# FFN2 in column groups of 256 and 512 in a fused attention and FFN kernel, with the bursts and the loads reordered

## The chip, the cores and the metric

The kernel runs on one core of a Trainium2 chip. The core has a matrix engine (TensorE, PE in the profile; its weight loads are listed as PEld), a vector engine (VectorE, DVE), a scalar engine (ScalarE, ACT), a general engine (GpSimd, POOL) and a sync engine (SP). In this kernel POOL only starts loads, and SP only starts transposes and the writes of the output. The metric is the time of one execution on the device in microseconds (us), lower is better; the time before is 387.18 us, the median of four runs from 386.85 to 387.43.

## What is computed

The reference is an attention without softmax, followed by a feed-forward network with a leaky activation:

```python
scores = (q @ k^T) / sqrt(64)                # 8 batches, 12 heads, 448 x 448
attn   = maximum(scores, 0)**2 / 448
x      = concat_heads(attn @ v)              # 3584 tokens x 768
h      = x @ w_in                            # 768 -> 2048
g      = maximum(h, 0) + alpha * minimum(h, 0)
out    = g @ w_out                           # 2048 -> 768, float32
```

All inputs are float32 in HBM. The loads that POOL starts convert to bfloat16 on the way, and the matrix products are done in bfloat16 with float32 sums.

## The kernel before

**Attention in quads.** Four heads of one batch make a quad; there are 24, three to a batch, numbered 0 to 23. `load_qk` (L93) and `load_v` (L102) bring a quad's q, k and v into SBUF through POOL. q and k must then be turned so that the head's 64 dimensions lie along the partitions. For quads 0 to 4 `turn_pe` (L148) does it with TensorE; from quad 5 on `turn_dma` (L160) does it: two DVE copies reorder q and k into a tile `perm`, then one DMA transpose issued by SP writes the tile `T`. The raw tiles of q and k have three buffers each, so a load of quad n waits until the tiles of quad n - 3 have been turned.

A quad's scores come in seven chunks. `score_mm` (L172) runs four matmuls of 64 x 64 weights by 448 columns for a chunk, side by side in the four quarters of the array, into a pair of PSUM banks. `relu` (L183) takes the chunk out of PSUM on ACT or DVE, and `square` (L191) squares it in SBUF. `attnv` (L199) runs 28 matmuls, seven rounds of four, over the seven squared chunks, again into a pair of banks, and ACT (L216) and DVE (L217) each take one bank of it out, scaled, into `xT`.

**FFN1** (`f1_mm` L238, `f1_out` L244): for each batch, 16 blocks `ff` of 128 hidden features, six matmuls of 448 columns each. ACT makes the negative part (L248), DVE combines it with alpha into `gT` (L249). `gT` holds two batches, a superbatch `sb`, and has a single buffer.

**FFN2** (`f2`, L258): a unit is `(sb, c, h)`: 128 tokens of a superbatch (c from 0 to 6) and one half h of the 768 output columns. Sixteen matmuls, with the tokens' columns of `gT` as the weights and 384 columns of `w_out` streamed, sum into one bank. ACT copies the bank to SBUF (L265), and two DMAs write the rows, both issued by SP (L271); only the very last unit is split in two parts and uses the ACT queue for half of its writes. `w_out` is loaded in the same halves by `load_w_out` (L119), four DMAs a half.

**Banks.** PSUM has eight banks, given out in program order to whoever was longest ago: `take_bank` gives one bank (FFN1, FFN2), `take_pair` one of the four aligned pairs whose later use is the oldest (scores, A@V), and `hold` keeps a bank over a stretch of code. A matmul into a bank waits until the engine that empties the bank has read the last content.

**Order.** Nothing is scheduled by the compiler: each engine's queue runs in the order in which the program is written. Attention work is put between the units of the FFN. `run(some(3))` puts three score chunks in and squares what is waiting. A `burst(n)` (L405) is three score chunks, the A@V of quad n, two more chunks, and the squares. In a superbatch's first (even) batch the six units of c = 0 to 2 follow FFN1, and bursts stand before units 1, 3 and 5 of the list; in the odd batch eight units of c = 3 to 6 follow, with bursts before units 1, 4 and 7. The first superbatch is written out by hand (L279 to L454), with a few units of FFN2 placed between the scores of quads 4 and 5 and the rest between four runs and three bursts.

**The loads around the change.** POOL issues in order. Before the scores of quad 2 come the first half of `w_out`, q and k of quad 5 and v of quad 3 (L303 to L307). After FFN1 of batch 0 come `turn_dma(5)`, q and k of 6, and then `landed` (L373): a copy of one element of quad 5's `T`, so that POOL issues nothing further until this transpose has landed. Then q and k of 7 and 8, and v of 6 to 8. Quads 9 and 10 and the second half of `w_out` follow in FFN1 of batch 1 (L431 to L434), where quads 7 and 8 are turned too (L429, L430).

Of the kernel before, what the change touches and what calls it, by code (L numbers as in the profile page):

```python
# [20 lines left out]
def kernel(  # L21
# [15 lines left out]
    KM = d_model // 128  # L37
    KF = d_ff // 128
    NQ = B * NG
    HALF = d_model // 2  # L40
    out_scale = 1.0 / (D * S)

    ctx.enter_context(tc.manual_schedule())
# [12 lines left out]

    ident = singles.tile([128, 128], BF16)
    w_in_sb = singles.tile([128, NG, 2, d_ff], BF16)
    w_out_sb = singles.tile([128, 2, KF, HALF], BF16)
    alpha_sb = singles.tile([128, KF], F32)  # L60
    beta_sb = singles.tile([128, KF], F32)
    landed = singles.tile([1, 1], BF16)
# [30 lines left out]
    def load_qk(n, names="qk"):  # L93
        b, g = divmod(n, NG)
        for name in names:
            src = q if name == "q" else k
            t = raw_pool.tile([128, 2, NJ, D], BF16, tag=name, name=f"{name}raw")
            flat = src[b].rearrange("(m two) (pp j) d -> (two pp) m (j d)", two=2, j=NJ)
            nc.gpsimd.dma_start(out=t.rearrange("p m j d -> p m (j d)"), in_=flat[:, 2 * g:2 * g + 2])  # L99
            raw[(n, name)] = t  # L100
# [6 lines left out]
        vraw[n] = t  # L107

    w_in_v = moe_w_in.rearrange("(g hf e pp) f -> hf e pp g f", hf=2, e=2, pp=64)
    w_out_v = moe_w_out.rearrange("(kf p) (h c) -> h p kf c", p=128, h=2)  # L110

    def load_w_in(i):
        lo, hi = 512 * i, 512 * i + 512
# [4 lines left out]

    def load_w_out(h, lo=0, hi=KF, step=4):  # L119
        for lo in range(lo, hi, step):  # L120
            nc.gpsimd.dma_start(out=w_out_sb[:, h, lo:lo + step], in_=w_out_v[h][:, lo:lo + step])

    FIRST = 4
    first, flat0 = {}, {}
# [106 lines left out]
    def run(chunks):  # L231
        sc(chunks)
        sq()


    gT = {}
# [18 lines left out]
        f1_mm(ps, b, ff, range(KM))  # L255
        f1_out(ps, b, ff)

    def f2(sb, c, hf, parts=((0, HALF),)):  # L258
        o = o_pool.tile([128, HALF], F32, tag="o", name="osb")
        for lo, hi in parts:  # L260
            ps = take_bank()[:, :hi - lo]
            for ff in range(KF):
                nc.tensor.matmul(ps, gT[sb][:, ff, bass.ts(c, 128)], w_out_sb[:, hf, ff, lo:hi],  # L263
                                 start=(ff == 0), stop=(ff == KF - 1))
            nc.scalar.copy(o[:, lo:hi], ps)  # L265
            for u in range(2):
                blk = 2 * c + u
                b, j = 2 * sb + blk // NJ, blk % NJ
                rows = out[b * S:(b + 1) * S].rearrange("(pp j) d -> j pp d", j=NJ)
                eng = nc.scalar if u and hi - lo < HALF else nc.sync  # L270
                eng.dma_start(out=rows[j][:, hf * HALF + lo:hf * HALF + hi], in_=o[64 * u:64 * u + 64, lo:hi])  # L271


    pat = "ADAAAAA"
# [25 lines left out]
    sq(1)  # L300
    sc([(1, 4, "D"), (1, 5, "A"), (1, 6, "A")])
    sq(2)
    load_w_out(0, 0, 12)  # L303
    load_qk(5, "q")
    load_w_out(0, 12)
    load_qk(5, "k")
    load_v(3)  # L307
    early = {}
    todo = []

# [29 lines left out]
    def f1s(b, lo, hi):  # L340
        for ff in range(lo, hi):
            f1(b, ff)
# [20 lines left out]
    f1_out(ps, 0, 9)  # L363
    f1s(0, 10, 12)
    sc(ch(3, 6, 7) + ch(4, 0, 2, "AA"))
    f1s(0, 12, 14)
    kept = late[:]
    del late[:]
    f1s(0, 14, 16)
    turn_dma(5)  # L370
    late += kept
    load_qk(6)
    nc.gpsimd.tensor_copy(landed, T[5][:1, 0, 0, :1])  # L373
    load_qk(7)
    load_qk(8)
    load_v(6)
    load_v(7)
    load_v(8)
    f2(0, 0, 0)
    sq()  # L380
    sc(ch(4, 2, 5, "AAADAAA"))
# [3 lines left out]
    sq(2, "A")  # L385
    sq()
    turn_dma(6)
    f2(0, 1, 0)
    f2(0, 2, 0)
    sc(ch(5, 0, 3))  # L390
# [31 lines left out]
    for ff in range(KF):  # L422
        if ff < 5:
            f1_mm(psum[:, early[ff], :S], 1, ff, range(4, KM))
            f1_out(psum[:, early[ff], :S], 1, ff)
            take(early[ff], 1)
        else:
            f1(1, ff)
        if ff in (1, 4):  # L429
            turn_dma(7 + ff // 3)  # L430
        if ff == 6:  # L431
            load(9)
            load(10)
# [12 lines left out]
    burst(6)  # L446
    f2(0, 2, 1)
    f2(0, 3, 1)
    prepare(10)
    burst(7)  # L450
    f2(0, 4, 1)
    f2(0, 5, 1)
    burst(8)
    f2(0, 6, 1)  # L454

    for b in range(2, B):
        n0 = NG * (b + 1)
        last = b == B - 1
        sb = b // 2
        for ff in range(KF):  # L460
            if not last and ff in (6, 12):
                run(some(3))
            if not last and ff in (1, 9):
                prepare(n0 + 2 + ff // 8)
            f1(b, ff)
        if b % 2 == 0:
            units = [(sb, c, h) for c in range(3) for h in range(2)]
            at = {1: 0, 3: 1, 5: 2}
        else:
# [12 lines left out]

# [29 lines left out]
```

## The time and the profile before

| what | before |
|---|---|
| median of four runs | 387.18 us |
| the profiled execution | 387.0 us |
| its span, first to last instruction | 385.0 us |
| TensorE busy | 376.8 us, 98% |
| VectorE busy | 266.0 us, 69% |
| ScalarE busy | 205.3 us, 53% |
| read from HBM / written | 45.62 MB / 11.01 MB |
| mean granted TensorE clock | 0.999 |

The profile is one execution recorded by the hardware. Busy time is the time in which an engine had an instruction in work; matmuls overlap each other, so a busy TensorE can still lose time between them. Rows of groups read: source line, engine, operation, output <- inputs, shape, count, then busy time and the mean of one, then the idle time before them and what ended it. Rows of the chain of work that ended last and of the timeline begin with the start and the length in us, and consecutive instructions of one kind are merged into one row. In the timeline the square brackets give the idle time of the engine before the row. Rows of a table by stretch begin with the two ends and the length of the stretch and end with the granted clock, the mean busy share of the 16 DMA engines and GB/s. A name such as SPq or ACTq stands for the part of an engine that issues DMAs. A DMA's time to landing is counted from its issue to its last completion signal.

### The profile page before, as it was taken

To read this page: it belongs to the slowest core of one execution; us is meant where nothing else is said; L and a number is where in the kernel's file an instruction comes from. 1 tells how busy PE (TensorE), PEld (TensorE's weight loads), DVE (VectorE), ACT (ScalarE), POOL (GpSimd) and SP (SyncE) were. 2 spreads that over 40 slices of the span, in tenths; PEclk is the share of its full clock that TensorE was granted. 3 is DMA by queue.
4 is the path that set the end of the run, shared out by engine and by line. 5 is a ranking of instruction groups with operands and counts; after the bars stand their busy time and mean duration, and the time that the engine had idled before them with its cause. 6 is when DMAs were issued, how large, how long until landed. Compare 5 with 4: busy or idle time off the path is not lost.

```text
span 385.0 us, 7861 instructions
## 1 busy us (share of the span) xinstructions
PE 376.8 (98%) x3200; PEld 210.5 (55%) x3200; DVE 266.0 (69%) x422; ACT 205.3 (53%) x331; POOL 67.9 (18%) x102
## 2 busy tenths in 40 slices
PE   7799999999999999999999999999999999999996
PEld 6444564555665456545555455654555545655564
DVE  4987877857768978788656887689754887626300
ACT  5978577536454754455444555547543475434311
POOL 8556234620102202022100221020000000000000
PEclk9999999999999999999999999999999999999999
DMA  9999999999993666688292772946036300120023
GB/s 159 191 203 204 203 161 206 177 191 221 155 188 63 108 116 101 119 125 119 45 180 55 128 122 42 181 69 120 22 74 99 70 0 23 43 61 2 13 71 82
DMA packets 73284, 43.42 MB, mean 113 GB/s; under 512 B 40352, under 2 KB 73248, under 8 KB 73248
## 3 DMA queue, kind: packets, MB, share of 16 engines
q0 software_dynamic: 26864, 22.45, 39.7%
q1 hardware_dynamic: 45952, 20.10, 26.1%
q8 instruction: 25, 0.41, 0.4%
q10 hardware_dynamic: 432, 0.36, 0.3%
q14 instruction: 11, 0.09, 0.1%
HBM read 45.62 MB, written 11.01 MB: 147 GB/s over the span
## 4 chain that ended last, share of the span: by engine, by line
PE 94%; DVE 3%; DMA 1%; ACT 0%; ACTq 0%; issue 0%
PE psum L240 38%; PE psum L263 38%; PE psum L177 9%; PE psum L206 8%; DVE at L196 2%; DMA qfirst<-in_q_dram 1%; PE psum L155 1%; DVE T L158 1%; DVE rl L188 1%; ACT osb L265 0%; ACTq L271 0%; DVE qraw L139 0%; ACT T L158 0%
## 5 line engine op out<-in xcount | busy, mean ns | idle before, releaser
L263 PE MATMUL psum<-w_out_sb,gT 128*128 128x384 bf16 (+2 forms) x912 | 151.0, 323 | 0.0
L240 PE MATMUL psum<-xT,w_in_sb 128*128 128x448 bf16 x768 | 149.9, 353 | 0.0
L263 PEld LDWEIGHTS <-gT 128*128 128x128 bf16 x912 | 86.8, 98 | 62.9 <-issue 8.2
L240 PEld LDWEIGHTS <-w_in_sb 128*128 128x128 bf16 x768 | 73.6, 98 | 72.3 <-issue 6.0
L249 DVE SCALAR_TENSOR_TENSOR gT<-neg,beta_sb,psum 128x448 bf16<-128x448 f32 x128 | 83.5, 677 | 31.6 <-ACT neg L248 31.6
L248 ACT ACTIVATE neg<-psum 128x448 f32<-128x448 f32 x128 | 69.2, 546 | 61.9 <-PE psum L240 59.1
L186 ACT ACTIVATE rl<-psum 128x896 bf16<-128x896 f32 x113 | 98.1, 934 | 1.6 <-PE psum L177 1.6
L196 DVE TENSOR_TENSOR at<-rl 128x896 bf16<-128x896 bf16 x164 | 91.7, 618 | 0.0
L188 DVE TENSOR_SCALAR rl<-psum 128x896 bf16<-128x896 f32 x55 | 59.7, 1086 | 43.5 <-PE psum L177 43.5
L265 ACT COPY osb<-psum 128x384 f32<-128x384 f32 (+2 forms) x57 | 26.9, 473 | 106.4 <-PE psum L263 106.4
L177 PE MATMUL psum<-T 64*64 64x448 bf16 x672 | 45.5, 356 | 3.0 <-DVE T L158 1.1
L99 POOL DMA_DIRECT2D qraw<-in_q_dram x23 | 16.6, 723 | 161.7 <-DVE perm L163 156.6
L206 PE MATMUL psum<-at,vraw 64*64 64x448 bf16 x672 | 37.4, 351 | 0.3 <-DVE at L196 0.2
L206 PEld LDWEIGHTS <-vraw 64*64 64x64 bf16 x672 | 24.4, 106 | 10.5 <-issue 2.4
L177 PEld LDWEIGHTS <-T 64*64 64x64 bf16 x672 | 18.2, 105 | 21.7 <-issue 14.9
L217 DVE TENSOR_SCALAR xT<-psum 128x448 bf16<-128x448 f32 x23 | 14.4, 624 | 15.6 <-PE psum L206 11.2
L106 POOL DMA_DIRECT2D vraw<-in_v_dram x24 | 17.5, 733 | 5.4 <-DMA kraw<-in_k_dram 2.8
L99 POOL DMA_DIRECT2D kraw<-in_k_dram x23 | 16.6, 723 | 3.4 <-DMA w_out_sb<-in_moe_w_out_dram 1.2
L216 ACT ACTIVATE xT<-psum 128x448 bf16<-128x448 f32 x23 | 12.6, 549 | 2.5 <-PE psum L206 2.5
L163 DVE COPY perm<-qraw 128x896 bf16<-128x896 bf16 x19 | 11.6, 612 | 0.0
L163 DVE COPY perm<-kraw 128x896 bf16<-128x896 bf16 x19 | 11.6, 609 | 0.0
L116 POOL DMA_DIRECT2D w_in_sb<-in_moe_w_in_dram x16 | 10.1, 633 | 6.9 <-DMA kraw<-in_k_dram 2.6
(25 smaller groups left out, 40.5 us busy)
## 6 DMA issues: line engine op xcount, KB each, us to landing
out_dram<-osb SPq DMA_DIRECT2D x110, 96.0 KB, 2.2
vraw<-in_v_dram POOLq DMA_DIRECT2D x24, 224.0 KB, 8.1
qraw<-in_q_dram POOLq DMA_DIRECT2D x23, 224.0 KB, 5.4
kraw<-in_k_dram POOLq DMA_DIRECT2D x23, 224.0 KB, 6.9
w_in_sb<-in_moe_w_in_dram POOLq DMA_DIRECT2D x16, 192.0 KB, 8.5
w_out_sb<-in_moe_w_out_dram POOLq DMA_DIRECT2D x8, 384.0 KB, 12.0
qfirst<-in_q_dram SPq DMA_DIRECT2D x1, 448.0 KB, 4.1
T<-perm SPq DMA_TRANSPOSE x19, 6.3
```

The source lines that it names most:

```text
L99: nc.gpsimd.dma_start(out=t.rearrange("p m j d -> p m (j d)"), in_=flat[:, 2 * g:2 * g + 2])
L163: nc.vector.tensor_copy(p[:, i], raw.pop((n, name)).rearrange("p s j d -> p j s d"))
L177: nc.tensor.matmul(ps[64 * c:64 * c + 64, r, :S], t[64 * r:64 * r + 64, 1, j, 64 * c:64 * c + 64], t[64 * r:64 * r + 64, 0, :, 64 * c:64 * ...
L186: nc.scalar.activation(rl, ps[:, :, :S], ACTF.Relu)
L188: nc.vector.tensor_scalar(rl, ps[:, :, :S], 0.0, None, ALU.max)
L196: nc.vector.tensor_tensor(a, rl, rl, ALU.mult)
L206: nc.tensor.matmul(ps[64 * s:64 * s + 64, r, :S], vv[64 * r:64 * r + 64, s, j, :], a[64 * r:64 * r + 64, s], start=(j == 0), stop=(j == NJ ...
L240: nc.tensor.matmul(ps, w_in_sb[:, km // 2, km % 2, bass.ts(ff, 128)], xT[b][:, km // 2, km % 2, :], start=(km == 0), stop=(km == KM - 1))
L248: nc.scalar.activation(neg, ps, ACTF.Relu, scale=-1.0)
L249: nc.vector.scalar_tensor_tensor(gT[b // 2][:, ff, (b % 2) * S:(b % 2) * S + S], neg, beta_sb[:, ff:ff + 1], ps, ALU.mult, ALU.add)
L263: nc.tensor.matmul(ps, gT[sb][:, ff, bass.ts(c, 128)], w_out_sb[:, hf, ff, lo:hi], start=(ff == 0), stop=(ff == KF - 1))
L265: nc.scalar.copy(o[:, lo:hi], ps)
```

## The change

The 768 output columns are no longer cut in the middle but at 256: h = 0 now means the first 256 columns, h = 1 the other 512. Everything that follows the cut changes with it: the two tiles of `w_out`, their loads (rows of 1024 and 2048 bytes in HBM instead of 1536), the output tile's width and the length of ACT's copies. The last unit is split into 384 and 128 columns instead of 256 and 128.

The order of units is changed so that the unit right before every burst is one of 256 columns. In even batches that holds by itself; in odd batches two pairs of units are swapped; in the first superbatch the list is rewritten, with the same seven interruptions.

The loads are moved: two of the four pieces of the first `w_out` tile now follow q and k of 5 and v of 3; `turn_dma(5)` stands ahead of FFN1's ff = 12 instead of behind ff = 15; q of quad 7 is issued ahead of the `landed` gate; the 512-column tile of `w_out` is loaded behind k of 7 and q and k of 8, ahead of v of 6; q and k of 9 and v of 7 to 9 follow `turn_dma(6)`; `turn_dma(8)` moves from ff = 4 to ff = 10 of batch 1, and quad 10's loads to ff = 1.

```diff
-    HALF = d_model // 2
+    CUT = d_model // 3
+    COLS = ((0, CUT), (CUT, d_model))
...
-    w_out_sb = singles.tile([128, 2, KF, HALF], BF16)
+    w_out_sb = [singles.tile([128, KF, hi - lo], BF16, name=f"w_out{i}") for i, (lo, hi) in enumerate(COLS)]
...
-            nc.gpsimd.dma_start(out=w_out_sb[:, h, lo:lo + step], in_=w_out_v[h][:, lo:lo + step])
+            nc.gpsimd.dma_start(out=w_out_sb[h][:, lo:lo + step], in_=w_out_v[:, lo:lo + step, COLS[h][0]:COLS[h][1]])
...
-    def f2(sb, c, hf, parts=((0, HALF),)):
-        o = o_pool.tile([128, HALF], F32, tag="o", name="osb")
-        for lo, hi in parts:
+    def f2(sb, c, h, parts=None):
+
+        first_col, width = COLS[h][0], COLS[h][1] - COLS[h][0]
+        o = o_pool.tile([128, d_model - CUT], F32, tag="o", name="osb")
+        for lo, hi in parts or ((0, width),):
...
-    load_w_out(0, 0, 12)
-    load_qk(5, "q")
-    load_w_out(0, 12)
-    load_qk(5, "k")
+    load_w_out(0, 0, 8)
+    load_qk(5)
     load_v(3)
+    load_w_out(0, 8)
...
-    f1s(0, 12, 14)
+    turn_dma(5)
+    f1s(0, 12, 13)
     kept = late[:]
     del late[:]
-    f1s(0, 14, 16)
-    turn_dma(5)
+    f1s(0, 13, 16)
     late += kept
     load_qk(6)
+    load_qk(7, "q")
     nc.gpsimd.tensor_copy(landed, T[5][:1, 0, 0, :1])
-    load_qk(7)
+    load_qk(7, "k")
     load_qk(8)
+    load_w_out(1)
     load_v(6)
-    load_v(7)
-    load_v(8)
     f2(0, 0, 0)
...
     turn_dma(6)
+    load_qk(9)
+    load_v(7)
+    load_v(8)
+    load_v(9)
     f2(0, 1, 0)
     f2(0, 2, 0)
...
-        if ff in (1, 4):
-            turn_dma(7 + ff // 3)
-        if ff == 6:
-            load(9)
+        if ff in (1, 10):
+            turn_dma(7 + ff // 9)
+        if ff == 1:
             load(10)
-            load_w_out(1)
     f2(0, 3, 0)
-    run(some(3))
-    f2(0, 4, 0)
-    f2(0, 5, 0)
-    prepare(9)
-    run(some(3))
-    f2(0, 6, 0)
     run(some(3))
     f2(0, 0, 1)
     run(some(3))
     f2(0, 1, 1)
+    f2(0, 2, 1)
+    prepare(9)
+    run(some(3))
+    f2(0, 4, 0)
     burst(6)
-    f2(0, 2, 1)
     f2(0, 3, 1)
+    run(some(3))
+    f2(0, 4, 1)
+    f2(0, 5, 0)
     prepare(10)
     burst(7)
-    f2(0, 4, 1)
     f2(0, 5, 1)
+    f2(0, 6, 0)
     burst(8)
     f2(0, 6, 1)
...
-            units = [(sb, c, h) for c in range(3, 7) for h in range(2)]
+            units = [(sb, 3, 0), (sb, 3, 1), (sb, 4, 1), (sb, 4, 0), (sb, 5, 1), (sb, 5, 0), (sb, 6, 0), (sb, 6, 1)]
...
-                f2(*u, parts=((0, 256), (256, HALF)))
+                f2(*u, parts=((0, 384), (384, 512)))
```

More of the change, by code (lines that the diff above doesn't have):

```diff
@@ L109 @@
     w_in_v = moe_w_in.rearrange("(g hf e pp) f -> hf e pp g f", hf=2, e=2, pp=64)
-    w_out_v = moe_w_out.rearrange("(kf p) (h c) -> h p kf c", p=128, h=2)
+    w_out_v = moe_w_out.rearrange("(kf p) c -> p kf c", p=128)
     def load_w_in(i):
@@ L256, in f1 @@
         f1_out(ps, b, ff)
-    def f2(sb, c, hf, parts=((0, HALF),)):
-        o = o_pool.tile([128, HALF], F32, tag="o", name="osb")
-        for lo, hi in parts:
+    def f2(sb, c, h, parts=None):
+        first_col, width = COLS[h][0], COLS[h][1] - COLS[h][0]
+        o = o_pool.tile([128, d_model - CUT], F32, tag="o", name="osb")
+        for lo, hi in parts or ((0, width),):
             ps = take_bank()[:, :hi - lo]
             for ff in range(KF):
-                nc.tensor.matmul(ps, gT[sb][:, ff, bass.ts(c, 128)], w_out_sb[:, hf, ff, lo:hi],
+                nc.tensor.matmul(ps, gT[sb][:, ff, bass.ts(c, 128)], w_out_sb[h][:, ff, lo:hi],
                                  start=(ff == 0), stop=(ff == KF - 1))
@@ L269, in f2 @@
                 rows = out[b * S:(b + 1) * S].rearrange("(pp j) d -> j pp d", j=NJ)
-                eng = nc.scalar if u and hi - lo < HALF else nc.sync
-                eng.dma_start(out=rows[j][:, hf * HALF + lo:hf * HALF + hi], in_=o[64 * u:64 * u + 64, lo:hi])
+                eng = nc.scalar if u and parts else nc.sync
+                eng.dma_start(out=rows[j][:, first_col + lo:first_col + hi], in_=o[64 * u:64 * u + 64, lo:hi])
     pat = "ADAAAAA"
```

## The prediction

> **What bounds the kernel now.** I read the page first: busy times, then the chain that ended last.
>
> ```profile
> PE 376.8 (98%) x3200; PEld 210.5 (55%) x3200; DVE 266.0 (69%) x422; ACT 205.3 (53%) x331; POOL 67.9 (18%) x102
> PEclk9999999999999999999999999999999999999999
> PE 94%; DVE 3%; DMA 1%; ACT 0%; ACTq 0%; issue 0%
> L263 PE MATMUL psum<-w_out_sb,gT 128*128 128x384 bf16 (+2 forms) x912 | 151.0, 323 | 0.0
> ```
>
> TensorE is the bound at full clock: 376.8 of 385.0 us. A change here can win only what lies between useful matmuls, and lose whatever makes TensorE wait. So the next view is the chain in order of time, for the rate of a stream and the length of each interruption.
>
> ```profile
> 61.84 1.45 PE psum L206 x28
> 81.12 0.69 PE psum L177 x12
> 118.01 6.81 PE psum L240 x36
> 137.76 2.60 PE psum L263 x16
> 148.82 1.39 PE psum L206 x28
> ```
>
> A 448-column matmul costs 6.81/36 = 0.189 us, a 384-column one 2.60/16 = 0.1625. A run of 12 score matmuls (three rounds of four that run side by side) takes 0.69 = 3 x 0.189 + 0.12; an A@V standing alone (seven rounds) takes 1.45 = 7 x 0.189 + 0.13. So an interruption costs its rounds plus about 0.125. A whole burst (12 scores, A@V, 8 scores: twelve rounds) should then take 12 x 0.189 + 0.125 = 2.395. The timeline says otherwise:
>
> ```profile
> 140.29 0.76 PE L177 MATMUL psum<-T 64*64 64x448 bf16 x12
> 140.40 0.48 ACT L265 COPY osb<-psum 128x384 f32<-128x384 f32 x1 [2.06 <-PE psum L263]
> 140.93 1.52 PE L206 MATMUL psum<-at,vraw 64*64 64x448 bf16 x28
> 142.76 0.34 PE L263 MATMUL psum<-w_out_sb,gT 128*128 128x384 bf16 x1
> ...
> 148.06 0.76 PE L177 MATMUL psum<-T 64*64 64x448 bf16 x12
> 148.17 0.48 ACT L265 COPY osb<-psum 128x384 f32<-128x384 f32 x1 [2.12 <-PE psum L263]
> 148.65 1.56 PE L206 MATMUL psum<-at,vraw 64*64 64x448 bf16 x28
> 150.52 0.34 PE L263 MATMUL psum<-w_out_sb,gT 128*128 128x384 bf16 x1
> ```
>
> The two bursts take 142.76 - 140.29 = 2.47 and 150.52 - 148.06 = 2.46: some 0.065 too much. The cause is in the ACT rows. Following take_pair and take_bank by hand, the pair of banks that A@V takes always holds the bank of the FFN2 group just before the burst. ACT's copy of that group ends at 140.88 and 148.65; in the first burst A@V starts 0.05 after it, 0.64 behind the first score instead of 0.59. In the second it starts on time in one bank, and the matmuls of the other bank start 0.05 after the copy, so the four array quarters run 0.07 out of step to the end. The wait list does not name it, since it counts only gaps in which TensorE is empty.
>
> **The change part by part.**
>
> *Groups of 256 and 512.* The tail has a 256-column group, and ACT's copies time the groups:
>
> ```profile
> 376.29 0.48 ACT L265 COPY osb<-psum 128x384 f32<-128x384 f32 x1 [2.12 <-PE psum L263]
> 378.89 0.48 ACT L265 COPY osb<-psum 128x384 f32<-128x384 f32 x1 [2.12 <-PE psum L263]
> 380.64 0.37 ACT L265 COPY osb<-psum 128x256 f32<-128x256 f32 x1 [1.27 <-PE psum L263]
> 381.04 0.55 ACTq L271 DMA_DIRECT2D out_dram<-osb  x1
> ```
>
> 384 columns: 378.89 - 376.29 = 2.60; 256: 380.64 - 378.89 = 1.75, or 0.109 each. The line through 0.109 and 0.1625 puts 512 at 0.216, 3.45 a group; the 448-column row lies on it. 1.75 + 3.45 = 5.20 = 2 x 2.60. There are 28 such pairs and 912 matmuls before and after, so the stream changes by 0. ACT: 0.37 + 0.58 (512 on the same line) against 2 x 0.48, nothing. The 112 issues on SP and the bytes written stay.
>
> *Bursts behind a 256-column group.* The copy becomes 0.37, so it ends 0.11 + 0.37 = 0.48 after the first score, and with the 0.05 of latency the banks are free at 0.53; A@V comes at 0.59. The wait goes, with 0.06 to spare. What is next late in a burst: the fourth score chunk needs the relu of the first, which ended at 149.46 for a start at 149.98, and now ends 0.1 earlier: covered. The first lap keeps its seven interruptions (four runs, three bursts) in a new order, and behind the same banks. The chain shows 19 bursts of this kind (the A@V rows of 1.39): quads 3, 4, 6 to 22. Bounds: 0 if something else holds A@V, 19 x 0.07 = 1.33; I take 19 x 0.066 = **-1.26**, as both forms of the wait are visible.
>
> *First FFN2 group after FFN1, eight times.* Its last matmul comes after 15 x 0.109 = 1.64 instead of 2.44, its weight load after 1.53. It needs the last gT tile:
>
> ```profile
> 138.38 0.68 DVE L249 SCALAR_TENSOR_TENSOR gT<-neg,beta_sb,psum 128x448 bf16<-128x448 f32 x1 [0.28 <-ACT neg L248]
> ```
>
> Group start is 137.60, so gT is done at 1.46, and with 0.05 latency at 1.51. The cover shrinks from about 0.8 to 0.02. Bounds 0 and 8 x 0.1; I take 0, as DVE ran without a backlog there.
>
> *The end.* The split of the last group puts a 384-column copy (0.48 for 0.37) before the ACT-queue issue of 0.55 that the last copy stands behind: **+0.1**.
>
> *Loads and the transpose of quad 5.* Three groups before quad 5's scores shrink by 0.85 and burst 3 by 0.07, so TensorE asks for T of quad 5 at 55.57 - 2.63 = 52.94. In the old kernel:
>
> ```profile
> 48.07 2.35 SPq L165 DMA_TRANSPOSE T<-perm  x1
> 54.28 0.18 POOL L373 COPY landed<-T 1x1 bf16<-1x1 bf16 x1 [10.81 <-DMA T<-perm]
> 67.53 15.57 SPq L165 DMA_TRANSPOSE T<-perm  x2
> ...
> 48.00:50.00 2.00, 1.00 1.27 203
> 50.00:52.00 2.00, 1.00 1.48 134
> 52.00:54.00 2.00, 1.00 1.06 264
> ```
>
> It landed at about 54.2, 1.35 before use. The change moves the two DVE copies (0.61 each) ahead of gT 12, into a DVE gap from 42.2 to 43.4, so SP issues at about 43.3. The k of quad 5 must be in by then: it landed 34.57 + 12.7 = 47.3 behind four w_out pieces of 384 KB, and now stands behind two of 256 KB; 1.05 MB less at 203 GB/s is 5.2 us, 42.1, against a DVE need of 42.7. At 43.3 the POOL queue is still full: four pieces and eight quad tiles (q of 7 is now ahead of the gate) are 2.88 MB against 3.18 MB. The old loads ended at about 50.7 (0.8 MB moved from 50 to 54, less 0.46 of T and 0.2 of output). So they now end at 49.3 if bytes count, at 51.8 if a 512-byte row takes as long as a 768-byte one. Landing: at best 49.3 + 0.46 MB at 264 GB/s = 51.0, at worst 51.8 + the 3.5 that T took after the old loads = 55.3. That is a stall of 0 to 2.4. I take 53.2, **+0.3**: the rows from 67.53 on show transposes and loads moving together, so part of T is moved before the loads end.
>
> The old row by itself (nothing of T before 50, when loads ran low) gives 50.6 + 3.5 = 54.1, a stall of 1.2 and 387.2 in all. The Trainium skill (DMA: Bandwidth & Descriptors, section "Queues, rings and completion order") says that an engine alternates between the queues that have work, packet by packet; by that T shares from its issue, an estimate of no stall and 386.0. No row here shows which holds for this queue depth.
>
> *w_out's 512 columns.* 2 MB behind the gate instead of after FFN1's ff 6. Issued from about 54, behind three tiles and beside quad 6's transpose: 2.8 MB at 150 GB/s (191 shared, less the transpose) ends near 73; first use is 78.3. v of 6 follows, needed at 92. Quads 7 and 8: T at 89.5 and 98, issued by 65 and 73; the worst rows are 15.7 and 19.6 us. Moving the two copies for quad 8 from ff 4 to ff 10 lets six gT tiles pass them on DVE and puts 1.2 us before later ones, where DVE has a gap of some 0.46 in each 1.13 and ff 11 to 15 to catch up. On SP the same transpose comes after quad 7's, as before; the tiles of 7 to 9 are read by DVE only when long landed. Covered, 0. Between 47 and 63 DVE had 0.5 + 2.0 + 1.3 idle and loses the 1.1 of the copies moved, against 2.6 by which TensorE comes earlier: 0.
>
> Sum: -1.26 + 0.1 + 0.3 = -0.86. The profiled execution took 387.0 (span 385.0 and 2.0 around it), so 386.1; the median is 0.18 above it: **386.3**.
>
> **The rivals.**
> 1. *T of quad 5 comes late.* Place: the first scores of quad 5, with TensorE empty. It eats the gain once T lands 1.16 after 52.94, and the kernel is slower by 0.2% from a landing at about 54.9. For it: the 15.7 of the next transpose under a full queue, which from 43.3 would be 59.0; against: the gate stops the loads. At 56: 387.2 - 1.16 + 3.1 = 389.1.
> 2. *The bursts keep 2.46*, because the stagger is not the copy's. For it: the wait list shows nothing; against: 0.05 behind the copy in both forms. 387.2 + 0.4 = 387.6.
> 3. *The early w_out delays v or transposes* past 78.3: 388 to 390. Against: 5 us of cover.
>
> **How the numbers follow.** A difference under 0.2% (0.77 us) is about what a measurement of this kernel can't tell from none. Forecast 0.70, its own range 385.8 to 386.9 (stall 0 to 0.8): 0.50 below 386.4, 0.20 above. Rival 2: 0.12, of it 0.10 same and 0.02 slower. Rivals 1 and 3: 0.15 and 0.03, slower. Faster 0.50, same 0.30, slower 0.20. The range 385.7 to 388.0 leaves out most of rivals 1 and 3.
>
> **What would show it.** Bursts of 2.40 and A@V 0.59 behind the first score; FFN2 groups of 1.75 and 3.45; no gap in the first group after FFN1; a gap of 0 to 0.8 before quad 5's scores near 52.9. A TensorE gap over 1 us near 53 or 78, or bursts of 2.46, would make the forecast wrong.

## The result, and the profile after

The changed kernel takes 386.53 us (median of 31 runs, 385.92 to 388.81) against 387.31 us for the kernel before (49 runs, 386.84 to 388.52). The ratio is 0.9984, 95% interval 0.9978 to 0.9990: 0.16% less, real by its interval. The two medians lie 0.78 us apart, 0.20%, which is just the size that the prediction called the edge of what a measurement tells. A second series on another occasion gave 386.24 (7 runs) against 387.32 us (24 runs), ratio 0.9973 (0.9963 to 0.9984). The forecast was 386.3 us. In all series together two executions, one of the kernel before (397.16 us) and one of the kernel narrow_tail below (392.41 us), were in a slow state and are left out of the comparisons.

The profiled execution took 386.16 us with a span of 384.2 us, 0.80 less than before. From its page, the busy times, the two lines of the chain that ended last, and the largest group:

```profile
PE 375.8 (98%) x3200; PEld 205.6 (54%) x3200; DVE 266.0 (69%) x422; ACT 206.9 (54%) x331; POOL 67.8 (18%) x102
PE 92%; DMA 4%; DVE 3%; ACT 0%; issue 0%; ACTq 0%
PE psum L241 38%; PE psum L266 37%; PE psum L178 9%; PE psum L207 8%; DMA T<-perm 3%; DVE at L197 2%; DMA qfirst<-in_q_dram 1%; PE psum L156 1%; DVE T L159 1%; DVE rl L189 1%; ACT osb L268 0%; ACTq L274 0%; ACT T L159 0%; DVE qraw L140 0%
L266 PE MATMUL psum<-w_out,gT 128*128 128x256 bf16 (+3 forms) x912 | 150.9, 323 | 0.0
```

TensorE is the bound as before, and the FFN2 stream is as long as before (150.9 us against 151.0, same count and mean). New in the chain is `DMA T<-perm` with 3%: in this execution a transpose ended last once. The timeline of the two bursts that were shown of before (start, length, engine, work; in brackets what the engine idled for):

```profile
139.50 0.76 PE L178 MATMUL psum<-T 64*64 64x448 bf16 x12
139.60 0.37 ACT L268 COPY osb<-psum 128x256 f32<-128x256 f32 x1 [1.20 <-PE psum L266]
140.09 1.49 PE L207 MATMUL psum<-at,vraw 64*64 64x448 bf16 x28
141.90 5.37 PE L266 MATMUL psum<-w_out,gT 128*128 128x512 bf16 x32
...
147.20 0.76 PE L178 MATMUL psum<-T 64*64 64x448 bf16 x12
147.31 0.37 ACT L268 COPY osb<-psum 128x256 f32<-128x256 f32 x1 [1.16 <-PE psum L266]
147.79 1.49 PE L207 MATMUL psum<-at,vraw 64*64 64x448 bf16 x28
149.59 0.60 PE L266 MATMUL psum<-w_out,gT 128*128 128x512 bf16 x2
```

Both bursts take 2.40 us, from 139.50 to 141.90 and from 147.20 to 149.59, and A@V comes 0.59 us behind the first score. ACT's copy is over at 139.97 and 147.68, 0.1 us before A@V wants the banks. All 19 bursts together take 45.35 us in the trace, where they took 46.61: 1.26 us won. The chain shows the groups:

```profile
76.21 1.75 PE psum L266 x16
77.96 0.69 PE psum L178 x12
78.65 3.56 PE psum L266 x16
147.96 1.32 PE psum L207 x28
```

A group of 256 columns takes 1.75 us; within the one of 512 the matmuls follow at 0.216 us (16 x 0.216 = 3.46, and 0.1 to the work behind it). The A@V row, 1.39 us before, is 1.32. And the transpose of quad 5, from the chain and the timeline:

```profile
43.44 9.84 DMA T<-perm
...
53.32 0.76 PE L178 MATMUL psum<-T 64*64 64x448 bf16 x12 [0.20 <-DMA T<-perm]
53.34 0.18 POOL L376 COPY landed<-T 1x1 bf16<-1x1 bf16 x1 [10.48 <-DMA T<-perm]
...
q0 software_dynamic: 267, 0.22, 91.6%
q1 hardware_dynamic: 257, 0.07, 32.3%
```

(The last two lines are the DMA queues from 47.5 to 49.0 us: packets, MB and share. q0 holds POOL's loads, q1 the transfers that SP issues, here packets of T.) It was issued at 43.44 and landed at 53.28; from the last FFN2 matmul to the first score of quad 5 it is 0.468 us, where it is 0.203 in a profile without a wait there: a wait of 0.27. The end, from the timeline:

```profile
379.76 0.48 ACT L268 COPY osb<-psum 128x384 f32<-128x384 f32 x1 [2.23 <-PE psum L266]
380.27 0.55 ACTq L274 DMA_DIRECT2D out_dram<-osb  x1
380.86 0.27 ACT L268 COPY osb<-psum 128x128 f32<-128x128 f32 x1 [0.62 <-PE psum L266]
```

By starts in the two traces the 0.80 us divide so: the first FFN2 group starts at 45.22 us instead of 45.10 (+0.12, ahead of any changed unit); from there to the last stretch of FFN2 it takes 314.39 us instead of 315.39 (-1.00 = -1.26 of the bursts + 0.27 of quad 5's wait, rounded); from there to the last copy 21.25 instead of 21.14, and to the end of the span +0.08 in all.

In this series the changed kernel scatters more from run to run: a standard deviation of 0.62 us in 31 runs against 0.30 in 49. In the second series it does not: 0.25 us in 7 runs against 0.27 in 24.

### The profile page after: what moved, and what is told of

It reads as the page before. It is cut to its first block, busy times and chain, and to the rows that moved or that the text cites. A ratio compares the mean times of both kernels' runs of the same rounds, so it can differ in the third digit from the quotient of the medians.

```text
span 384.2 us, 7860 instructions
## 1 busy us (share of the span) xinstructions
PE 375.8 (98%) x3200; PEld 205.6 (54%) x3200; DVE 266.0 (69%) x422; ACT 206.9 (54%) x331; POOL 67.8 (18%) x102
## 4 chain that ended last, share of the span: by engine, by line
PE 92%; DMA 4%; DVE 3%; ACT 0%; issue 0%; ACTq 0%
PE psum L241 38%; PE psum L266 37%; PE psum L178 9%; PE psum L207 8%; DMA T<-perm 3%; DVE at L197 2%; DMA qfirst<-in_q_dram 1%; PE psum L156 1%; DVE T L159 1%; DVE rl L189 1%; ACT osb L268 0%; ACTq L274 0%; ACT T L159 0%; DVE qraw L140 0%
## 5 line engine op out<-in xcount | busy, mean ns | idle before, releaser
L266 PE MATMUL psum<-w_out,gT 128*128 128x256 bf16 (+3 forms) x912 | 150.9, 323 | 0.0
L268 ACT COPY osb<-psum 128x256 f32<-128x256 f32 (+3 forms) x57 | 27.0, 473 | 104.4 <-PE psum L266 98.7
L178 PE MATMUL psum<-T 64*64 64x448 bf16 x672 | 44.7, 356 | 3.2 <-DVE T L159 1.1
L207 PE MATMUL psum<-at,vraw 64*64 64x448 bf16 x672 | 36.6, 350 | 0.3 <-DVE at L197 0.2
L178 PEld LDWEIGHTS <-T 64*64 64x64 bf16 x672 | 16.6, 105 | 21.7 <-issue 12.5
L207 PEld LDWEIGHTS <-vraw 64*64 64x64 bf16 x672 | 20.9, 106 | 12.6 <-issue 2.3
```

What stands on the lines that cost most here:

```text
L178: nc.tensor.matmul(ps[64 * c:64 * c + 64, r, :S], t[64 * r:64 * r + 64, 1, j, 64 * c:64 * c + 64], t[64 * r:64 * r + 64, 0, :, 64 * c:64 * ...
L207: nc.tensor.matmul(ps[64 * s:64 * s + 64, r, :S], vv[64 * r:64 * r + 64, s, j, :], a[64 * r:64 * r + 64, s], start=(j == 0), stop=(j == NJ ...
```

## The experiments

Every run had the kernel before beside it on the same chip. Theory: the bursts gain because the copy ahead of A@V is short, and the moved loads bring nothing by themselves. Rivals: the gain is the loads'; the stagger in A@V is not the copy's. Later runs ask what T of quad 5 and `w_out` cost, and where the scatter is from. Each kernel has a short name, given with its measured time.

### The loads alone

The kernel before, with the moved loads and turns of the change, and halves of 384 columns in the old order.

```diff
-    load_w_out(0, 0, 12)
-    load_qk(5, "q")
-    load_w_out(0, 12)
-    load_qk(5, "k")
+    load_w_out(0, 0, 8)
+    load_qk(5)
     load_v(3)
+    load_w_out(0, 8)
...
+    turn_dma(5)
-    f1s(0, 12, 14)
+    f1s(0, 12, 13)
...
+    load_w_out(1)
     load_v(6)
```

> The kernel before with the moved loads and transposes alone: two halves of 384 columns and the old order of units. Theory: bursts stay at 2.46; T of quad 5 lands at about 53.5 and is asked for at 55.6, so nothing waits, and the time is 387.2, no difference. Rival (the gain comes from the earlier loads): 386.4 to 386.6, as the changed kernel.

Measured (loads_only): 387.85 us (387.23 to 388.61, eight runs) against 387.18, ratio 1.0022 (1.0012 to 1.0031). The 19 bursts take 46.60 us, as before. So the loads don't carry the gain; alone they lose. The timeline shows where:

```profile
45.49 2.11 PE L263 MATMUL psum<-w_out_sb,gT 128*128 128x384 bf16 x12
48.48 0.81 PE L263 MATMUL psum<-w_out_sb,gT 128*128 128x384 bf16 x4 [0.88 <-DMA w_out_sb<-in_moe_w_out_dram]
```

The first unit ran out of `w_out` after 12 of 16 matmuls: the spacing there is 1.21 us instead of 0.16, 1.05 lost. With 384 columns the pieces now behind quad 5 and v of 3 are half as large again as the 256-column pieces of the change, which had no such gap. T of quad 5 landed at 56.72, not near 53.5 as expected; the scores of quad 5 did not wait for it, since the first unit's stall had pushed them back to 56.99.

### The copy made shorter, loads and order as before

The kernel before with its loads and its order; only the unit ahead of a burst is computed as 256 and then 128 columns, each part with a bank, a copy and writes of its own (the loop's units shown; the five written out by hand likewise).

```diff
+    NARROW = ((0, 256), (256, HALF))
...
-                f2(*u)
+                f2(*u, parts=NARROW if i + 1 in at and not last else ((0, HALF),))
```

> The kernel before, its loads, its order and its 384 columns unchanged; only the FFN2 unit ahead of each of the 19 bursts is computed as 256 and then 128 columns, each with its own PSUM bank, copy and output transfers. The copy ahead of the A@V is then that of 128 columns, about 0.26 us against 0.48, and TensorE has 16 matmuls more for each burst, 16 x 2.5 ns = 0.04 us. The theory (the burst pays for what the last copy lasts beyond the three score chunks, 0.066 us with 384 columns and nothing with 256 or less) expects bursts of 2.40 us, as in the changed kernel, none of the early waits of the changed loads, and 387.2 - 19 x (0.066 - 0.04) = 386.7 us. The rival (A@V still waited a few hundredths behind the copy of 256 columns, so that a shorter copy brings more) expects bursts of 2.34 us and 385.7 us. If the bursts stayed at 2.46 us the copy wouldn't be what they wait for, and the time would be 388.0 us.

Measured (narrow_tail): 386.86 us (386.50 to 387.42, ten runs) against 387.32, ratio 0.9990 (0.9981 to 1.0000). A burst and the group before it, from the timeline:

```profile
95.15 2.81 PE L263 MATMUL psum<-w_out_sb,gT 128*128 128x256 bf16 x32
97.89 0.76 PE L177 MATMUL psum<-T 64*64 64x448 bf16 x12
98.00 0.27 ACT L265 COPY osb<-psum 128x128 f32<-128x128 f32 x1 [0.52 <-PE psum L263]
98.49 1.49 PE L206 MATMUL psum<-at,vraw 64*64 64x448 bf16 x28
100.29 0.50 PE L263 MATMUL psum<-w_out_sb,gT 128*128 128x384 bf16 x2
```

The burst takes 2.40 us (97.89 to 100.29), all 19 together 45.35 us, to the hundredth the sum of the changed kernel. The group grew from 2.70 to 2.74, the 0.04 that was expected. The parts take other banks than the whole group did, but `take_bank` and `take_pair` followed through the program still give each of these A@V a pair that holds the bank of the last copy, as in the kernel before and in the changed one; so the wait did not go because A@V got another bank. A copy of 0.27 us thus brings no more than one of 0.37: the theory holds, and the wait is gone at 256 columns. The median fell by 0.46 us, with 0.5 expected. In the profiled execution another wait took 0.24 back, in the first unit of all. Its chain, and then VectorE's timeline around the first unit in the kernel before and in the changed kernel:

```profile
45.61 0.54 DVE at L196
46.15 1.20 DVE gT L249 x2
...
47.39 1.18 PE psum L263 x17
...
45.65 1.27 DVE L249 SCALAR_TENSOR_TENSOR gT<-neg,beta_sb,psum 128x448 bf16<-128x448 f32 x2
...
44.65 2.04 DVE L250 SCALAR_TENSOR_TENSOR gT<-neg,beta_sb,psum 128x448 bf16<-128x448 f32 x3
```

The first group of 256 columns needed the last tile of `gT` before DVE had made it. In the kernel before, this tile is done at 46.92, 1.82 us after the first group's start (45.10), and so it is in narrow_tail; a group of 256 columns wants it at 1.64. After the other seven FFN1 it is done at 1.46, the figure that the prediction took for all eight. In the changed kernel the first one, too, is done at 1.46 (46.69 for a start at 45.22): the change keeps one more square back (`f1s(0, 12, 13)` for `f1s(0, 12, 14)`), and without a square in between DVE makes the last three tiles in a row.

### Every burst behind 512 columns

The changed kernel with the cut at 512, so that h = 0 is the wide part and precedes each burst.

```diff
-    CUT = d_model // 3
+    CUT = 2 * d_model // 3
```

> The changed kernel with the cut at 512, so that the first tile of w_out has 512 columns and the second 256; every burst then follows a 512-column unit, and the last unit is split in 128 and 128. All else as in the changed kernel. Theory (the length of ACT's copy sets A@V's start): the copy takes 0.59 instead of 0.37, A@V comes 0.11 + 0.59 + 0.05 = 0.75 behind the first score instead of 0.59, each burst takes 2.55 to 2.56, and the time is 386.5 + 19 x 0.16 - 0.3 (no wait for quad 5's T, which is asked for 5 us later) = 389.2. Rival (what counts is only that the columns are cut in 256 and 512, or the earlier loads): 386.2 to 386.6.

Measured (wide_first): 394.06 us (391.95 to 395.77, four runs), ratio 1.0180 (1.0153 to 1.0207); the profiled execution was the shortest, with a span of 390.1 us. One burst from its timeline:

```profile
152.17 0.76 PE L178 MATMUL psum<-T 64*64 64x448 bf16 x12
152.27 0.58 ACT L268 COPY osb<-psum 128x512 f32<-128x512 f32 x1 [3.08 <-PE psum L266]
152.76 1.66 PE L207 MATMUL psum<-at,vraw 64*64 64x448 bf16 x28
154.73 0.94 PE L266 MATMUL psum<-w_out,gT 128*128 128x256 bf16 x7
...
50.30 1.02 PE L266 MATMUL psum<-w_out,gT 128*128 128x512 bf16 x4 [1.80 <-DMA w_out<-in_moe_w_out_dram]
```

This burst takes 2.56 us, and A@V runs out of step for 1.66 us instead of 1.49; in 12 of the 19 bursts all of A@V starts late, 0.74 behind the first score. The 19 take 48.64 us, 3.29 more than in the changed kernel. With narrow_tail this gives the burst as a function of the copy: 0.27 or 0.37 us, 2.40; 0.48 us, 2.46; 0.58 us, 2.56 to 2.57. The rest of the loss was not expected: the first unit now needs the large tile, which is not there (two gaps, 2.2 us in all; the larger stands in the last row). What the other three runs lost beyond the profiled one, 2.0 to 3.6 us of span, no trace shows; their mean granted clock was 0.989 to 0.996, that of the profiled one 0.998.

### The copy shared by two engines

The kernel before; the copy ahead of a burst is done half by ACT and half by DVE.

```diff
-            nc.scalar.copy(o[:, lo:hi], ps)
+            if share:
+                mid = (hi - lo) // 2
+                nc.scalar.copy(o[:, lo:lo + mid], ps[:, :mid])
+                nc.vector.tensor_copy(o[:, lo + mid:hi], ps[:, mid:])
+            else:
+                nc.scalar.copy(o[:, lo:hi], ps)
```

> The kernel before, its 384-column units and its loads, with one edit: the copy of each unit right before a burst is shared, 192 columns by ACT and 192 by DVE. Theory: each half takes about 0.32, both banks are free 0.48 behind the first score, A@V comes at 0.59, each burst takes 2.40, and with the old slack for quad 5's T the whole 1.25 is won: 386.0. Rival (the gain of the change is not the copy): 387.2, or later if DVE's extra 0.3 per burst holds up the relus behind it.

Measured (split_copy): 394.60 us (394.09 to 396.31, five runs), ratio 1.0206 (1.0189 to 1.0224). A burst from the timeline:

```profile
142.22 0.76 PE L177 MATMUL psum<-T 64*64 64x448 bf16 x12
142.33 0.32 ACT L267 COPY osb<-psum 128x192 f32<-128x192 f32 x1 [2.06 <-PE psum L263]
142.68 0.36 DVE L268 COPY osb<-psum 128x192 f32<-128x192 f32 x1 [1.69 <-ACT osb L267]
142.96 1.08 DVE L188 TENSOR_SCALAR rl<-psum 128x896 bf16<-128x896 f32 x1
143.09 1.52 PE L206 MATMUL psum<-at,vraw 64*64 64x448 bf16 x28
```

The halves did not run side by side: the profile names ACT's half as what DVE's waited for, so the bank is free at 143.04, 0.82 after the first score, and A@V starts 0.05 behind that, at 0.87. The expectation failed, but on the same rule: A@V starts 0.05 us behind the end of the copy or 0.59 behind the first score, whichever is later. (That holds for the 10 bursts in which the copied bank is the first of A@V's pair; in the other 9 A@V starts at 0.59 and its matmuls into the second bank come late.) The longer bursts (53.88 us for 19, 7.28 more than before) make up the time; DVE's relu also begins later.

### Quad 5's transpose: gate and place

First, q of quad 7 put behind the gate again, so that fewer loads are ahead of the transpose:

```diff
-    load_qk(7, "q")
     nc.gpsimd.tensor_copy(landed, T[5][:1, 0, 0, :1])
-    load_qk(7, "k")
+    load_qk(7)
```

> The changed kernel, with q of quad 7 issued behind the gate again, so that 224 KB less stand in the load queue ahead of quad 5's transpose. Theory (the gain is A@V's wait for ACT's copy, 19 x 0.066 = 1.25 us, and part of it goes to the wait for quad 5's T, 0.27 us in the profile): T lands about 1.1 us earlier, at 52.2, before TensorE asks for it at 53.1, so the gap of 0.27 goes, bursts stay at 2.40, and the time is 386.2, with a scatter as small as before's. Rival (the transpose's landing is set by something other than the bytes ahead of it): T lands at 53.3 again, 386.5.

Measured (gate_q7): 387.39 us (385.91 to 391.34, 12 runs), ratio 1.0018 (0.9994 to 1.0043). In its profile T of quad 5 is no longer late (it landed at 52.59, with 52.2 expected), but another load is. From the chain:

```profile
58.18 24.32 DMA w_out<-in_moe_w_out_dram
...
82.55 1.02 PE psum L266 x4
```

The last piece of the 512 columns needed 24.3 us and landed at 82.5, where it landed at 76.5 in the changed kernel; the first group of 512 columns stood still for 1.23 us. So what the prediction's third rival was about, the early `w_out` tile coming late, exists; it stands behind a load order that differs by one tile. Three of the 12 runs took 390 us or more. Their granted clock was 0.995 to 0.996, that of the others 0.998 or more, and none of them was profiled, so what they lost isn't known.

Second, the turn of quad 5 put back behind FFN1's last groups:

```diff
-    turn_dma(5)
     f1s(0, 12, 13)
...
     f1s(0, 13, 16)
+    turn_dma(5)
```

> The changed kernel with the turn of quad 5 (two copies on VectorE and the DMA transpose on SP) back behind the last groups of the first FFN1, where it stood before. All else as changed. The theory (the shorter FFN2 groups bring the scores of quad 5 forward by some 3 us, to 53 us, and T must land by then) expects the transpose to be issued near 48 us and to land near 54.2 us as in the kernel before, a wait of 1.0 to 1.3 us ahead of the scores of quad 5, and 387.4 us: moving the turn is then what keeps the gain. The rival (the transpose waits for the queue of loads to run empty, wherever it is issued) expects the landing near 53.2 us again, a wait of 0.3 us at most, and 386.4 us.

Measured (old_turn): 387.98 us (386.47 to 389.19, eight runs), ratio 1.0018 (1.0001 to 1.0034), some 1.4 us more than the changed kernel in its first series. But the profile (of a run of 387.14 us) shows other causes than the one expected:

```profile
46.46 0.61 DVE L164 COPY perm<-qraw 128x896 bf16<-128x896 bf16 x1
46.99 0.61 DVE L164 COPY perm<-kraw 128x896 bf16<-128x896 bf16 x1
48.59 1.08 DVE L189 TENSOR_SCALAR rl<-psum 128x896 bf16<-128x896 f32 x1
49.72 0.38 PE L178 MATMUL psum<-T 64*64 64x448 bf16 x4 [0.52 <-DVE rl L189]
52.80 0.18 POOL L376 COPY landed<-T 1x1 bf16<-1x1 bf16 x1 [9.99 <-DMA T<-perm]
...
107.37 0.38 PE L178 MATMUL psum<-T 64*64 64x448 bf16 x4 [0.37 <-DMA T<-perm]
```

T was issued at 47.69, 4.25 us later than in the changed kernel, and landed at 52.74, 0.54 us sooner and before its use at 53.64. So the earlier place of the turn does not bring the landing forward; there the rival was right. What it brings is seen at 49.72: here the two copies of the turn stand in DVE's queue ahead of a relu, which frees its banks late, a score chunk waits, and that burst takes 3.11 us instead of 2.40. At 107.37 a score chunk waits for T of quad 9, which landed at 107.32 (103.27 in the changed kernel), and that burst takes 2.96 us. These 1.27 us, less the 0.27 that the changed kernel waited for T of quad 5, are the 0.97 us by which the profiled span is longer, to a few hundredths. Neither theory nor rival had these two waits. The remaining 0.8 us of the median are in executions that were not profiled.

### Is the scatter w_out's?

Three kernels were to give the 512 columns more room. The changed kernel, beside the first two of them:

> The changed kernel once more, as the measure for the runs beside it. Both theories expect the median of its runs so far, 386.5 us, against 387.2 to 387.3 for the kernel before. The theory (the 512 columns of w_out land only some microseconds ahead of their use, and T of quad 5 some tenths behind it, so that a landing a little later is paid for in full) expects times between 385.9 and 388 us, spread about twice as wide as the kernel before. The rival (the spread is noise that belongs to no transfer) expects the same spread in the two runs beside it.

Measured (after_again): 386.24 us (386.02 to 386.78, seven runs), and no wait for T of quad 5 in the profile. The wide spread that was expected did not come. Without the loads of quad 8:

```diff
-    load_qk(8)
+    raw[(8, "q")], raw[(8, "k")] = raw[(7, "q")], raw[(7, "k")]
     load_w_out(1)
```

> The changed kernel without the loads of q and k of quad 8: quad 8 is computed from q and k of quad 7, so the output for that quad is another, and the two transfers of some 1.5 us each that stand ahead of w_out's 512 columns in the queue are gone. Everything else stands. The theory expects w_out's last piece to land near 73.5 us instead of 76.5 (82.5 in the run with q of 7 behind the gate), no wait in the first group of 512 columns in any run, a spread as narrow as that of the kernel before (nine runs of ten within 0.8 us), and a median of 386.2 us, which is the low end of the changed kernel's runs: the late landing of w_out is then worth 0.3 us of its median. The rival (the spread has nothing to do with w_out) expects the median and spread of the changed kernel, 386.5 and 1.3 us.

Measured (no_qk8): 386.10 us (385.89 to 386.66, six runs). The last piece landed at 75.0, as in the changed kernel beside it, and not at 73.5. The two loads were gone, but k of 7 and quad 6's transpose landed later (62.1 and 62.6 us instead of 58.4 and 60.4), and the first piece at 65.3 in both; why is open. With the units reordered:

```diff
     f2(0, 3, 0)
     run(some(3))
-    f2(0, 0, 1)
+    f2(0, 4, 0)
     run(some(3))
+    f2(0, 0, 1)
     f2(0, 1, 1)
...
-    f2(0, 5, 1)
-    f2(0, 6, 0)
+    f2(0, 4, 1)
+    f2(0, 5, 1, parts=((0, 256), (256, 512)))
     burst(8)
```

> The changed kernel, whole, with the units behind the second FFN1 in another order: the group of 256 columns of token chunk 4 runs second instead of sixth, so that the first group of 512 columns comes one group of 256 (1.75 us) later. The burst of quad 8 then has no group of 256 columns left ahead of it and follows one of 512 columns that is computed as 256 and 256 (16 matmuls more, 16 x 2.5 ns = 0.04 us). The loads are as in the changed kernel. The theory expects w_out's last piece to have 6.4 us to spare instead of 4.6, most of the waits for it gone, the spread back near 0.8 us and a median of 386.2 to 386.3 us. The rival expects 386.5 us and the changed kernel's spread.

Measured (late_wide): 386.65 us (386.09 to 388.54, 11 runs), ratio 0.9988 (0.9977 to 1.0000); 0.38 us more than in the changed kernel stands in the closing steps (last section). With the gate moved forward by some 3 us:

```diff
     attnv(3)
+    nc.gpsimd.tensor_copy(landed, xT[1][:1, 0, 1, :1])
+    load_qk(7, "k")
+    load_qk(8)
+    load_w_out(1)
+    load_v(6)
```

> The changed kernel with the gate of the load queue on another event: GpSimd's one-element copy waits for the scaled A@V of quad 3 (near 49.9 us) and no longer for T of quad 5 (53.3 us); k of 7, q and k of 8, the 512 columns of w_out and v of 6 are issued behind it as before, 3.4 us sooner. The theory (a load's first packets come 4 us or more behind its issue, so that the transpose of quad 5 is through by then) expects T of quad 5 at 53.1 to 53.4 us as in the changed kernel, w_out's last piece near 73 us instead of 75 to 76.5, and a time no worse than the changed kernel's: 386.2 us. The rival (packets of the loads come between those of the transpose) expects T of quad 5 to land a microsecond or more later, and 387.5 us or more.

Measured (gate_av): 386.45 us (386.15 to 387.53, 11 runs), ratio 0.9987 (0.9978 to 0.9996). Its timeline:

```profile
50.34 0.18 POOL L380 COPY landed<-xT 1x1 bf16<-1x1 bf16 x1 [7.27 <-DVE xT L218]
50.82 0.72 POOL L100 DMA_DIRECT2D kraw<-in_k_dram  x1 [0.30 <-issue]
53.53 0.76 PE L178 MATMUL psum<-T 64*64 64x448 bf16 x12
```

Quad 5's scores begin 0.06 us late although loads were issued from 50.8 on, and the last piece of `w_out` landed at 72.0. That is what the theory said of the transfers, but the time did not follow: in the profile the way from the first FFN2 group to the last stretch is 0.20 us shorter than in the changed kernel (314.19), while the first group starts later (45.64) and the last write lands 0.37 us later behind the last copy. In none of the four profiles does TensorE wait for `w_out`, the medians lie within 0.55 us of each other, and late_wide's highest run is nearly as far out as the highest of the changed kernel. So the theory that `w_out` makes the changed kernel's scatter is not supported. It is not refuted either, since the changed kernel itself did not scatter in that series (0.25 us); late_wide, beside it, did (0.65 us). What the profiles do show of `w_out` is the wait in gate_q7.

### The end, and a last version

The last two units exchanged, so that the last is one of 256 columns:

```diff
+            if last:
+                units[6:] = [(sb, 6, 1), (sb, 6, 0)]
...
-                f2(*u, parts=((0, 384), (384, 512)))
+                f2(*u, parts=((0, 128), (128, 256)))
```

> The changed kernel with its last two units exchanged: the last unit is the one of 256 columns, computed as 128 and 128, where it was the one of 512 columns, computed as 384 and 128. The copy that the ScalarE queue makes ahead of its output transfer is then one of 128 columns (0.27 us) and not of 384 (0.48 us), so that queue is free when the last copy may start. The theory expects the last copy to start 0.1 us sooner behind the start of the last FFN2 stretch, and a median 0.1 us under the changed kernel's, 386.2 to 386.4 us; that is less than the times can tell, and the trace decides. The rival (what comes last is the transfers' own landing, which the shorter copy doesn't move) expects the same time from the start of the last FFN2 stretch to the last landing as in the changed kernel.

Measured (tail_256): 386.62 us (386.37 to 386.94, 11 runs), ratio 0.9987 (0.9978 to 0.9996).

```profile
378.87 0.59 ACT L268 COPY osb<-psum 128x512 f32<-128x512 f32 x1 [3.08 <-PE psum L266]
379.48 2.63 SPq L274 DMA_DIRECT2D out_dram<-osb  x4
380.66 0.27 ACT L268 COPY osb<-psum 128x128 f32<-128x128 f32 x1 [0.63 <-PE psum L266]
```

The last copy starts 0.21 us sooner behind the start of the last stretch, and yet the end comes 0.43 later: from that copy to the end of the span it is 3.94 us against 3.30. SP now issues the two large writes of the unit of 512 columns just ahead of its two small ones, four issues from 379.48 to 382.11, and its last write starts at 381.57 instead of 381.15. Both the theory and the rival missed that queue. wide_first, whose last two units stand in the same way, has 3.94 us there too. The same exchange together with a gate on the output copy of the unit before:

```diff
-    nc.gpsimd.tensor_copy(landed, T[5][:1, 0, 0, :1])
...
-    f2(0, 1, 0)
+    f2(0, 1, 0, gate=True)
+    load_qk(7, "k")
```

> The changed kernel with the gate on the output copy of the unit ahead of the scores of quad 5 by one (near 52.6 us, 0.9 us sooner than T of quad 5 lands), and with the exchange of the last two units. The theory expects w_out's 512 columns about a microsecond sooner, T of quad 5 where it was, the last copy 0.1 us sooner, and 386.2 us. The rival (the loads disturb the transpose even at this distance) expects 386.6 us or more, with a wait of over 0.5 us ahead of the scores of quad 5.

Measured (gate_tail): 386.85 us (386.24 to 387.85, 11 runs), ratio 0.9993 (0.9984 to 1.0002); the wait ahead of quad 5's scores is 0.07 us, the end again 3.95 us behind the last copy. No version tried is better than the changed kernel by more than the runs can tell.

## Why the prediction was right or wrong

- **The forecast.** 386.3 us against 386.53 and, in the second series, 386.24. Right, also in kind: the gain is real and at the edge of what a measurement tells. For the profiled execution the sum gave 386.1, and it took 386.16. The median then lies 0.37 us above that execution, where the prediction had added 0.18 from the kernel before; this is scatter, which it did not forecast.
- **The stream of FFN2, 0.** Right: 150.9 us against 151.0, groups of 1.75 and 16 x 0.216.
- **The bursts, -1.26.** Right to the hundredth: 46.61 to 45.35 us. That the copy is the cause is shown by narrow_tail, which leaves the loads, the order and the halves alone, shortens the last copy and gets the same 45.35, and from the other side by wide_first and split_copy.
- **First FFN2 groups after FFN1, 0.** Right for the changed kernel: no group shows a gap. The row of 1.46 us was read off one group and used for all eight; for the first it was 1.82 in the kernel before, and narrow_tail shows what that costs a group of 256 columns: 0.24. In the changed kernel it is 1.46 there too, by the square that is kept back, which the prediction did not count. So for this one group the 0 was luck.
- **The end, +0.1.** Right: 0.11 to the last copy, 0.08 to the end of the span.
- **T of quad 5, landing 53.2, +0.3.** It landed at 53.28, with a wait of 0.27, in the first profile. In four more profiles of kernels that are the same up to there the wait was 0, 0, 0.19 and 0.40, so the mean of five is 0.17 and the term was a little large. Rival 1 did not come in any of them. That the landing was met within 0.1 us is partly luck: 53.2 was picked between 51.0 and 55.3, and old_turn shows that the landing hardly follows the issue, which the working started from. The idea behind the pick holds: by the time the last packet of the loads started, at 51.88 (the late end of 49.3 to 51.8), 1145 of T's 1792 packets had started, and T landed 1.4 us later and not 3.5 (in the kernel before it was 2.1, since the loads' last packet there started at 52.13 and not near 50.7). The Trainium skill (DMA: Bandwidth & Descriptors, section "Queues, rings and completion order") says that an engine alternates between the queues that have work, packet by packet. The trace agrees where both have work: from 47.5 to 49.0 us there are 257 packets of T beside 267 of the loads. What was not so is the estimate made from it, that T shares from its issue on and nothing waits: T's first packet started at 47.43, 4.0 us behind the issue, and its packets are the smaller ones (0.07 MB against 0.22 in that stretch).
- **`w_out`'s 512 columns, 0.** Right in the changed kernel: no wait. The landing was put 3.5 us too early, though: 76.5, with 73 expected, 2.1 us ahead of the first use at 78.65. The cover is 4.7 us all the same, since the last of four pieces is wanted only behind 12 matmuls, at 81.2; that it comes out near the "5 us of cover" that spoke against rival 3 is luck. gate_q7 shows how soon it is used up: the last piece landed 6 us later. That the moved tile itself did it is not shown, since in old_turn, with the changed kernel's order of loads, it landed at 81.53.
- **Not in the sum:** the start, +0.12 in the profiled execution. The same code reached the first FFN2 group at 45.09 to 45.64 us in the profiles of the kernels that change nothing before it, so this is variation between executions. And the scatter, which was not predicted and is only partly explained: the start (0.5 us), T of quad 5 (0 to 0.40) and the closing steps (below) each move by some tenths in the profiles.

## What to carry to other kernels

When a run of matmuls that is often interrupted takes longer than its count says, follow which buffer each piece gets and put the buffer's release beside the piece's start; a wait of 0.07 us under running matmuls is in no list of waits, but 19 of them are 1.3 us, and a copy shortened from 0.48 to 0.37 us removed them all. Once the copy fits under the work that is there anyway, shortening it further (0.27 us) brings nothing. A reordering that brings compute forward by 2.6 us spends the slack of every load behind it, so write down what each load has to spare: here 0 us for T of quad 5, 4.7 for `w_out` and, for the last tile of `gT`, 0.02 by the prediction's count; each of them became a wait in some kernel here. Issuing a transfer sooner into a full queue need not bring it in sooner: the turn of quad 5, issued 4.25 us earlier, landed no earlier.

## What was not expected of the hardware

- **Transposes and loads that start together.** In the two profiles in which quad 6's transpose was issued 0.7 to 0.9 us behind the first load past the gate (old_turn, gate_q7) it landed at about 67 us and the last piece of `w_out` at 81.5 and 82.5. In six profiles in which it was issued from 0.4 us behind that load to 0.4 us ahead of it, it landed at 60 to 63 and the last piece at 75.0 to 76.5. A few tenths at the issue went with some 6 us at the landing. What in the queues does this was not tried, and with loads 3 us ahead (gate_av) the transpose was late (71.3) but `w_out` early (72.0).
- **The closing steps.** At the end SP waits for the writes' semaphores one after the other in a fixed order, 0.06 us each. late_wide issues two writes more, so that its last two writes fall on early places of that order and seven waits come behind the one that lands last; from the last copy to the end of the span it took 3.68 us where the changed kernel took 3.30, with the last landing equally far behind the copy (2.34 us). That is read off the traces and was not tested by a run of its own. gate_av took 3.68 too, but there the last landing itself came later, 2.71 us behind the copy.
- **Two engines on one PSUM bank.** In split_copy the second half of a copy always began after the first had ended (19 waits of DVE on ACT's half), so a shared copy took 0.71 us where one by ACT alone took 0.48. Whether the engines could do it side by side is open.
